# Linear attention and gated convolution FFN on one core: fp32 staging of k, half loads, a split last output tile

## The chip, the cores and the metric

The kernel runs on one core of one Trainium2 chip. The metric is the device time of one execution in microseconds (us); three runs of the kernel before gave a median of 182.67 us (182.66 to 183.72).

## What is computed

The inputs are q, k and v (8 batches, 8 heads, 576 rows, 64 columns, fp32), a norm weight, and the weights of a feed-forward block. The attention is linear, without a softmax, and its output goes through an RMS norm over the 64 columns of a head. The block is a product, a ReLU, a depthwise convolution of three taps along the sequence, a sigmoid gate and a second product.

```python
kv = np.einsum('bhsd,bhse->bhde', k, v)
out = np.einsum('bhsd,bhde->bhse', q, kv)
rms = np.sqrt(np.mean(out * out, axis=-1, keepdims=True) + 1e-06)
x = out / rms * g_norm                      # heads side by side: (8, 576, 512)
h = np.maximum(x @ w_in, 0.0)               # w_in 512 x 1024
conv_out = sum(conv_w[k] * hp[:, k:k + S, :] for k in range(3))   # hp: h padded by one row at each end
gate = 1.0 / (1.0 + np.exp(-conv_out))
result = (h * gate) @ w_out                 # w_out 1024 x 512
```

## The kernel before

**A written order.** The kernel is a list of steps, ORDER, one token for each; the tokens are walked in turn, and each calls a small function (an `@op`) that issues the step's instructions. After the walk the instructions of each engine are chained in the order in which they were issued, so that every engine runs its own in exactly that order, and also the DMA issues of POOL and SP. Across engines only data and buffers hold a step back. In a token such as `om.0.2.1@3` the name is the step, the numbers are its arguments, the digits behind `@` choose the buffer that a new tile takes, and `!A` or `!V` choose ACT (ScalarE) or DVE (VectorE) for a copy or a ReLU.

**Buffers.** There are four PSUM buffers of two banks (names with "a"), two SBUF buffers each for q, k, v and for h, five for o32, and a few for each of the other tiles. A tile that takes a used buffer waits until all readers of the tile before it have finished. Four "row" buffers hold output rows until they are stored.

**Loads.** POOL loads q, k and v from fp32 memory into bf16 tiles, with the cast in the DMA (`load`, L347 and L349); `Lq.b`, `Lk.b` and `Lv.b` load a whole batch, 576 KB as bf16, and `Lq.b.u` one half of it (u = 0 or 1, four heads each). `Li.j` loads a quarter of w_in, `Lo.i` a half of w_out. The first halves of batch 0 do not come this way: in `pre` (L244), SP loads them as fp32 into the tile `stg` (L249), and the steps `ca` (L373) cast them on ACT and DVE, one quarter each.

**Attention.** For batch b: `kv` is the product of k and v (whole, or one half), `kvc` its copy from PSUM to bf16, `qt` transposes one half of q on PE and `qc` copies it, `ot` gives the attention output for one half, `sq` its squares on ACT.

**Norm.** Batches 0 and 1 go tile by tile: `on` sums the squares with a matrix of ones, `nl` takes the reciprocal root on ACT, `mz` scales on DVE. The other batches go in pairs, 2 and 3, 4 and 5, 6 and 7 (groups 1, 2, 3): `oc` copies the output to fp32, `ss` sums the squares of both batches into one tile, `ln` takes the reciprocal root, `sl` splits it into two bf16 parts in four DVE instructions, `sp` spreads it with small matmuls, and `mu` scales (eight for a pair). ACT changes its function table between the root and the sigmoid.

**Feed-forward.** `hm` multiplies one batch with one block of 128 columns of w_in, over one half of x, with `re` as the ReLU; for the pairs 2/3 and 4/5, `ha` and `hb` do it over both batches at once (512 columns, and the 128 left over), with `rea` and `reb`. On DVE `ta` makes the two side taps, `aa` and `ab` add them up, `mg` multiplies h by the gate, in place; `sg` is the sigmoid on ACT. The convolution runs over batch 0, batch 1, pairs 2/3 and 4/5, batch 6 and batch 7 (chunks 0 to 5); `mg.5.1` is the last of its products. `om.p.k.i` is half of the second product (four of the eight blocks of 128 of the inner dimension) for output tile k of pair p. A tile is 128 or 256 output rows of 512 columns; for pair 3 tiles 2 to 6 are single, and tile 6 is the last. `ea` (L643) copies the finished tile to a row buffer and `st` (L647, L650) stores it from SP.

**Zero-matmuls.** `fi`, `fn`, `fq` and `fo` multiply zeros, into a PSUM tile that is overwritten later; they only keep PE busy in waits.

**Around the change.** At the start PE runs the zero-matmuls, transposes the first half of q of batch 0, forms the first half of kv, and then needs the second halves, which POOL casts in the order q, k, v. Batches 2 to 7 are loaded whole. `om.0.2.0` stands ahead of `ss.2` and `ss.3`, the statistics of batches 2 and 3. The last three PE steps are `om.3.6.1`, `om.3.4.0` and `om.3.6.0`, four matmuls of 512 columns each.

Of the kernel before, what the change touches and what calls it, by code (L numbers as in the profile page):

```python
# [59 lines left out]
HALF = [0, 1]  # L60
# [3 lines left out]
OMT = {0: [(0, 1), (2, 3), (4, 5), (6, 7), (8,)], 1: [(0, 1), (2, 3), (4, 5), (6, 7), (8,)], 2: [(0, 1), (2, 3), (4, 5), (6, 7), (8,)], 3: [(0, 1), (2, 3), (4,), (5,), (6,), (7,), (8,)]}  # L64
TAPS = 2
# [15 lines left out]
mg.0.0 hm.1.7.0@1 hm.1.6.0@3 hm.1.7.1 qc.2.0!V@1 hm.1.2.0@2 hm.1.2.1 ta.0.6@1 sg.0.3 ta.0.7 re.1.2!A hm.1.6.1 re.1.6!A
hm.1.1.0@0 hm.1.4.0@2 hm.1.4.1 hm.1.5.0@3 sg.0.2 re.1.7!A hm.1.5.1 Lo.0 aa.0.3 kv.2@1 ab.0.3 re.1.4!A sg.0.6 sg.0.7
hm.1.1.1 re.1.5!A mg.0.1 ta.1.6@0 hm.1.0.0@2 hm.1.0.1 Lk.3@1 ta.1.7 kvc.2!V aa.1.3 re.1.1!A re.1.0!A ot.2.0@1,3
sq.2.0@0 mg.0.3 Lv.3@1 ta.1.4@1 hm.1.3.0@0 ab.1.3 oc.2.0@4 sq.2.1@1 ta.1.5 hm.1.3.1 re.1.3!V oc.2.1 om.0.1.0@2 aa.1.2
sg.1.7 ab.1.2 sg.1.6 mg.1.3 ta.1.0@0 ta.1.1 ot.2.1@1,3 sq.2.2@2 oc.2.2@0 sg.1.4 oc.2.3 sq.2.3@3 om.0.0.0@0 kv.3@1
kvc.3!V aa.1.0 ab.1.0 ot.3.1@1,3 Lo.1 fo.3.384.3.3 om.0.1.1 sg.1.5 oc.3.2@1 mg.1.2 Lq.5@1 oc.3.3 ta.1.3@1 ta.1.2
aa.1.1 sg.1.1 sq.3.2@4 om.0.0.1 qt.3.0@1 ea.0.1!A@0 sg.1.0 ab.1.1 mg.1.0 Lv.4@0 qt.5.1@2 sq.3.3@5 sg.1.3 Lk.4@0
qc.5.1!V@3 qc.3.0!V@2 om.0.2.1@3 sg.1.2 ot.3.0@2,1 ea.0.0!A@1 st.0.0 mg.1.1 sq.3.1@6 sq.3.0@7 om.0.2.0 ss.2@0 ss.3
ea.0.2!V@2 ln.1@0 Lv.5@1 kv.4@0 kvc.4!A oc.3.1@2 oc.3.0 om.0.3.1@3 sl.1@0 sp.2.0.1@0 sp.2.1.0@1 mu.2.1.0@1 mu.2.0.1
sp.3.1.1@2 mu.3.1.1 om.0.3.0 sp.2.0.0@1 mu.2.0.0 sp.2.1.1@0 qt.5.0@2 ea.0.3!A@3 qc.5.0!A@1 mu.2.1.1 sp.3.0.1@3 Lk.5@1  # L90
kv.5@1 mu.3.0.1 kvc.5!A Lq.4@0 sp.3.0.0@0 mu.3.0.0 sp.3.1.0@2 ot.5.1@3,1 sq.5.3@0 fo.2.384.5.2 ha.1.2.0@0 Lk.6@0
oc.5.3@3 mu.3.1.0 ot.5.0@2,1 ha.1.2.1 sq.5.2@1 oc.5.2 ha.1.3.0@3 Lv.7@0 oc.5.1@4 ha.1.3.1 rea.1.2!V@1 oc.5.0 sq.5.1@2
# [34 lines left out]
def kernel(  # L127
# [116 lines left out]
    def pre():  # L244
# [3 lines left out]
        for x in "qkv":  # L248
            nc.sync.dma_start(out=T["stg"][:, "qkv".index(x)], in_=rows(x, 0, 0, 2))  # L249
# [459 lines left out]
```

## Time and profile before

| | |
|---|---|
| median of three runs | 182.67 us |
| the profiled execution | 182.64 us, its span (first to last instruction) 180.9 us |
| matmuls on PE | 2238, of which 288 are the second product (65.4 us busy) |
| mean granted TensorE clock | 0.997 |
| POOL's load queue | 15.38 MB, 51.4% of 16 DMA engines over the span |
| SP's queue (staging and stores) | 11.21 MB, 16.6% |
| the three staging transfers, 576 KB each | 3.7, 4.7 and 5.8 us from issue to landing |
| longest waits on POOL | q loads, 18.7 us for PE's transposes; v loads, 11.8 us for kv |

Times count from the span's start unless they are durations. Engines are PE (matmuls), PEld (its weight loads, beside PE), DVE, ACT, POOL and SP. A line such as L638 is the line that issued an instruction; copies and ReLUs are issued by helpers, so L218 and L220 (copies), L224 and L226 (ReLUs) and L349 (loads) stand for many steps, and the tile's name and shape tell which. A wait on the page is put down to what ended it last.

### The profile page before, as it was taken

Reading aid. Unit: us, or ns where it says so; the run is one execution under the profiler, and the core shown is the slowest. Engines: PE = TensorE matmul, PEld = TensorE weight load, DVE = VectorE, ACT = ScalarE, POOL = GpSimd, SP = SyncE. Lnnn points to the kernel's source line nnn. Section 1 sums busy time; section 2 is a strip of 40 time slices with the busy share of each in tenths; the row PEclk is TensorE's granted clock in tenths of the full one; section 3 lists DMA queues with packets and bytes.
Section 4 is the critical chain, followed back from the end, with each engine's and each line's share of the span. In section 5 each row is a group of like instructions: output and inputs, shape, how many; then the busy total and the mean of one; then the engine's idle time right before and its main releaser. Section 6 shows DMA issues by size and latency. Waiting matters only on the chain.

```text
span 180.9 us, 5152 instructions
## 1 busy us (share of the span) xinstructions
PE 169.5 (94%) x2238; PEld 93.6 (52%) x2238; DVE 153.0 (85%) x268; ACT 139.8 (77%) x196; POOL 27.5 (15%) x49
## 2 busy tenths in 40 slices
PE   7987998899899889999999999999999999999991
PEld 7734754576344444545545564443477754444440
DVE  2656899999996695699999999999999989998840
ACT  2447499999999658999999999995999955755302
POOL 6964165103111311300000000000000000000000
PEclk9999999999999999999999999999999999999998
DMA  5999999999999999999019000004330000550694
GB/s 191 269 189 204 199 207 210 205 207 208 206 209 207 257 207 209 208 203 157 6 71 332 6 4 2 4 0 174 118 120 0 0 0 4 198 208 0 232 364 158
DMA packets 20954, 26.91 MB, mean 149 GB/s; under 512 B 952, under 2 KB 15556, under 8 KB 20932
## 3 DMA queue, kind: packets, MB, share of 16 engines
q0 software_dynamic: 15152, 15.38, 51.4%
q1 hardware_dynamic: 5776, 11.21, 16.6%
q8 instruction: 17, 0.28, 0.6%
q14 instruction: 5, 0.04, 0.1%
q10 hardware_dynamic: 4, 0.00, 0.0%
HBM read 32.52 MB, written 9.44 MB: 232 GB/s over the span
## 4 chain that ended last, share of the span: by engine, by line
PE 46%; DMA 24%; ACT 13%; DVE 9%; POOL 3%; issue 2%; POOLq 0%; ACTq 0%
PE om_ps L638 20%; DMA v_sb<-in_v_dram 15%; PE h_ps L526 10%; PE h_ps L539 10%; DMA k_sb<-in_k_dram 9%; ACT sq L440 3%; DVE xT L510 2%; ACT h L224 2%; ACT o L218 2%; ACT taps L620 2%; PE kv_ps L387 2%; PE h_ps L554 2%; DVE taps L588 2%; DVE taps L582 1%; ACT L213 1%
## 5 line engine op out<-in xcount | busy, mean ns | idle before, releaser
L638 PE MATMUL om_ps<-w_out_sb,h 128*128 128x512 bf16 x288 | 65.4, 379 | 0.0
L620 ACT ACTIVATE taps<-taps,cw 128x576 bf16<-128x576 bf16 (+1 forms) x48 | 43.8, 942 | 9.4 <-DVE taps L588 9.3
L638 PEld LDWEIGHTS <-h 128*128 128x128 bf16 x288 | 27.3, 98 | 32.2 <-issue 1.2
L224 ACT ACTIVATE h<-h_ps 128x576 bf16<-128x576 f32 (+2 forms) x44 | 32.0, 767 | 4.0 <-PE h_ps L526 3.1
L526 PE MATMUL h_ps<-xT,w_in_sb 128*128 128x288 bf16 x256 | 33.7, 286 | 0.4 <-DVE xT L510 0.2
L539 PE MATMUL h_ps<-xT,w_in_sb 128*128 128x512 bf16 x128 | 29.8, 380 | 0.1
L526 PEld LDWEIGHTS <-w_in_sb 128*128 128x128 bf16 x256 | 24.5, 98 | 8.4 <-issue 1.3
L218 ACT ACTIVATE row<-om_ps 128x1024 f32<-128x1024 f32 (+1 forms) x16 | 14.1, 887 | 12.4 <-PE om_ps L638 12.3
L588 DVE TENSOR_TENSOR taps<-taps,h 128x1152 bf16<-128x1152 bf16 (+1 forms) x24 | 22.9, 955 | 0.5
L440 ACT ACTIVATE sq<-o_ps 128x576 bf16<-128x576 f32 x32 | 20.5, 670 | 3.8 <-PE o_ps L433 3.6
L582 DVE TENSOR_TENSOR taps<-taps 128x1152 bf16<-128x1152 bf16 (+1 forms) x24 | 23.0, 956 | 0.4
L626 DVE TENSOR_TENSOR h<-h,taps 128x1152 bf16<-128x1152 bf16 (+1 forms) x24 | 22.7, 951 | 0.0
L575 DVE TENSOR_SCALAR taps<-h,cw 128x576 bf16<-128x576 bf16 (+1 forms) x48 | 20.0, 417 | 1.6 <-ACT h L224 1.6
L576 DVE TENSOR_SCALAR taps<-h,cw 128x576 bf16<-128x576 bf16 (+1 forms) x48 | 20.3, 422 | 0.0
L510 DVE SCALAR_TENSOR_TENSOR xT<-o,cw,sp_ps 128x576 bf16<-128x576 f32 x24 | 17.9, 808 | 1.6 <-PE sp_ps L503 1.6
L539 PEld LDWEIGHTS <-w_in_sb 128*128 128x128 bf16 x128 | 11.8, 98 | 13.9 <-issue 1.4
L218 ACT ACTIVATE o<-o_ps 128x576 f32<-128x576 f32 x24 | 15.6, 687 | 0.0
L213 ACT ACT_TABLE_LOAD x8 | 10.3, 1283 | 2.1 <-issue 2.0
L349 POOL DMA_DIRECT2D q_sb<-in_q_dram x9 | 6.8, 752 | 25.5 <-PE qt_ps L412 18.7
L220 DVE COPY qT<-qt_ps 128x1152 bf16<-128x1152 bf16 x11 | 8.2, 753 | 1.9 <-PE qt_ps L412 1.9
L226 DVE TENSOR_SCALAR h<-h_ps 128x576 bf16<-128x576 f32 (+1 forms) x8 | 6.9, 870 | 2.9 <-PE h_ps L539 2.1
L220 DVE COPY row<-om_ps 128x1024 f32<-128x1024 f32 (+1 forms) x6 | 5.7, 956 | 4.1 <-PE om_ps L638 3.3
(75 smaller groups left out, 140.0 us busy)
## 6 DMA issues: line engine op xcount, KB each, us to landing
out_dram<-row SPq DMA_DIRECT2D x14, 512.0 KB, 3.4
q_sb<-in_q_dram POOLq DMA_DIRECT2D x6, 576.0 KB, 12.0
v_sb<-in_v_dram POOLq DMA_DIRECT2D x6, 576.0 KB, 13.5
k_sb<-in_k_dram POOLq DMA_DIRECT2D x6, 576.0 KB, 15.2
out_dram<-row SPq DMA_DIRECT2D x8, 256.0 KB, 2.3
w_in_sb<-in_moe_w_in_dram POOLq DMA_DIRECT2D x4, 256.0 KB, 10.2
w_out_sb<-in_moe_w_out_dram POOLq DMA_DIRECT2D x2, 512.0 KB, 17.9
q_sb<-in_q_dram POOLq DMA_DIRECT2D x3, 288.0 KB, 8.6
```

Source lines behind the costliest of these rows:

```text
L218: nc.scalar.activation(to, fr, AX.Copy)
L224: nc.scalar.activation(to, fr, AX.Relu)
L440: nc.scalar.activation(by_r(s), natural(T["ot", b, t][:, :S]), AX.Square)
L510: nc.vector.scalar_tensor_tensor(x_tile(b)[:, 2 * tp:2 * tp + 2, at], T["o32", b, tp][:, :, at], g_sb, T["sp", b, tp, e][:, :, :HS], op0=A ...
L526: nc.tensor.matmul(ps[:, e, :HS], w_in_sb[:, t, f * P:(f + 1) * P], x[:, t, e * HS:(e + 1) * HS], start=(t == 0), stop=(t == NT - 1))
L539: nc.tensor.matmul(ps[:, e], w_in_sb[:, t, f * P:(f + 1) * P], x[:, t, e * 512:(e + 1) * 512], start=(t == 0), stop=(t == NT - 1))
L576: nc.vector.tensor_scalar_mul(tap[:, 1, f % 2, :n, :S], h[:, f], cw[:, 2 * NF + f:2 * NF + f + 1])
L582: nc.vector.tensor_add(tap[:, 1, :, :n, :S], tap[:, 0, :, :n, 7:7 + S], tap[:, 1, :, :n, 1:1 + S])
L588: nc.vector.tensor_add(y, y, h[:, 2 * j:2 * j + 2])
L620: nc.scalar.activation(y, y, AX.Sigmoid, scale=scale)
L626: nc.vector.tensor_mul(h, h, T["tap", c, j][:, 1, :, :n, :S])
L638: nc.tensor.matmul(ps[:, j], h[:, f, m * P:(m + 1) * P], w_out_sb[:, f, :], start=first and f == 4 * i, stop=not first and f == 4 * i + 3)
```

## The change

There are four edits. First, the second half of k of batch 0 is loaded by SP as fp32 into a new staging tile, `stg2`, issued right behind the three transfers of `stg`, and cast by two more `ca` steps; the POOL load `Lk.0.1` is gone. Second, batches 1 to 5 are loaded in halves (batches 0 and 1 were before), and `kv` runs by halves for them; POOL issues 38 loads of q, k and v instead of 27. Third, the last output tile (pair 3, tile 6) is computed in two column halves: each takes all eight blocks of the inner dimension and 256 columns, and has its own copy and its own store. Fourth, the order of all steps is new. With it, the stores of pair 0's first four tiles go out in pieces of 256 KB, and two tokens `sw` (a function that was there and unused) make the next store wait for a load: `st.0.1` for k of batch 4, `st.0.2` for v of batch 6.

The diff, cut; of the order three places are shown: the start, the statistics of batches 2 and 3, and the end.

```diff
-HALF = [0, 1]
+HALF = [0, 1, 2, 3, 4, 5]
...
+FIRST = 'k'
+HALFOUT = (3, 6)
+STORES2 = [(0, 1), (0, 2), (0, 0), (0, 3)]
...
-pre@0,0,0 ca.q.0!V Lq.0.1 ca.q.1!V fi.36.128@1 fi.3.128@1 qt.0.0@0 qc.0.0!A@0 ca.k.0!V ca.v.0!V ca.v.1!A ca.k.1!V
-fi.1.512@2 fi.20.128@2 ct@1 fq.2.512.kv.0.0@2 fq.1.256.kv.0.0 kv.0.0 Lk.0.1 pc fi.3.512@0 fi.2.128@0 qt.0.1@3 Lv.0.1
-qc.0.1!V@1 kvc.0.0!A ot.0.0@0,2 sq.0.0@0 sq.0.1@1 Lq.1.1@1 fn.3.512.on.0.0@1 fn.2.128.on.0.0 on.0.0 nl.0.0@0 pn Li.2
-fn.1.512.on.0.1@3 on.0.1 nl.0.1 mz.0.1@0 Li.0 fo.2.384.0.0 kv.0.1@1 kvc.0.1!A fq.1.512.ot.0.1@3 fq.1.256.ot.0.1
...
+pre@0,0,0 ca.q.1!V ca.q.0!A fi.9.512@1 fi.1.128@1 qt.0.0@0 pn Lq.0.1 ca.k.1!V qc.0.0!A@0 Lv.0.1 ca.k.0!V fi.6.512@2
+fi.2.128@2 ct@1 ca.v.1!A ca.v.0!V fq.1.512.kv.0.0@2 fq.1.256.kv.0.0 kv.0.0 kvc.0.0!A fq.2.512.ot.0.0@3 ot.0.0@0
+sq.0.1@0 fn.3.512.on.0.1@2 fn.2.128.on.0.1 on.0.1 ca.k.2!V sq.0.0@1 pc Lq.1.0@1 nl.0.1@0 fo.1.384.0.0 qt.0.1@1
+qc.0.1!V@1 Li.2 on.0.0@2 ca.k.3!A mz.0.1@0 fo.3.384.0.0 kv.0.1@1 nl.0.0 kvc.0.1!V fq.2.512.ot.0.1@2 ot.0.1@0 qt.1.0@1
...
+qt.2.0@3 mz.1.1 nl.1.0 qc.2.0!A@4 fq.1.512.ot.1.1@1 fq.1.256.ot.1.1 ot.1.1@2 sq.1.3@6 mz.1.0 Lq.3.1@1 aa.0.3
+fo.2.384.1.2 kv.2.0@3 on.1.3@0 Lq.2.1 sq.1.2@7 kvc.2.0!A fo.2.384.1.3 on.1.2@3 nl.1.3@3 nl.1.2 fo.1.384.1.2 hm.1.6.0@0
...
-qc.5.1!V@3 qc.3.0!V@2 om.0.2.1@3 sg.1.2 ot.3.0@2,1 ea.0.0!A@1 st.0.0 mg.1.1 sq.3.1@6 sq.3.0@7 om.0.2.0 ss.2@0 ss.3
-ea.0.2!V@2 ln.1@0 Lv.5@1 kv.4@0 kvc.4!A oc.3.1@2 oc.3.0 om.0.3.1@3 sl.1@0 sp.2.0.1@0 sp.2.1.0@1 mu.2.1.0@1 mu.2.0.1
...
+om.0.2.1@3 ea.0.0!V@1 sq.3.0@6 sq.3.1@7 ss.2@2 ss.3 sg.1.2 sg.1.3 mg.1.1 ln.1@0 Lv.5.1@0 sl.1@0 oc.3.0@2 Lk.5.0@0
+om.0.2.0 Lk.5.1 kv.5.1@2 oc.3.1 qt.5.0@0 sp.3.0.1@1 kvc.5.1!V sp.2.0.0@2 ea.0.2!A@2 mu.3.0.1@1 mu.2.0.0 qc.5.0!A@4
+om.0.3.0@3 sp.2.1.1@1 mu.2.1.1 sp.2.1.0@0 sp.3.1.1@2 om.0.3.1 Lq.4.0 mu.2.1.0 mu.3.1.1 Lq.5.1 sp.3.1.0@1 sp.2.0.1@0
+Lv.5.0 mu.2.0.1 qt.5.1@2 ea.0.3!A@3 sp.3.0.0@3 mu.3.1.0 mu.3.0.0 qc.5.1!A@2 Lk.4.0@1 kv.5.0@0 kvc.5.0!A Lv.4.0@1
+Lk.4.1 qt.4.0@1 sw.k.4 st.0.1 qc.4.0!V@1 ot.5.1@2,0 sq.5.2@0 sq.5.3@1 ha.1.2.0@3 ha.1.2.1 ha.1.3.0@1 Lv.4.1 oc.5.2@3
+Lq.7@1 oc.5.3 rea.1.2!V@0 ot.5.0@2,0 oc.5.1@0 ha.1.3.1 rea.1.3!V hb.1.0@3 sq.5.0@2 oc.5.0 sq.5.1@3 kv.4.1@2 kvc.4.1!V
+reb.1.0!A kv.4.0@1 fq.1.256.ot.4.1@0 ot.4.1@2 kvc.4.0!A sq.4.2@4 oc.4.3@4 ta.2.2@0 Lv.6@0 sq.4.3@5 ha.1.0.1@3 oc.4.2
...
-om.3.3.1@2 sg.5.0 om.3.2.1@0 sg.5.2 mg.5.0 st.2.1 mg.5.1 om.3.3.0 om.3.2.0 ea.3.0!V@0 st.3.0 ea.3.3!V@1 ea.3.2!V@2
-om.3.5.0 om.3.4.1@1 st.3.1 st.3.2 st.3.3 om.3.6.1@2 ea.3.5!V@0 st.3.5 om.3.4.0 ea.3.4!A@3 st.3.4 om.3.6.0 ea.3.6!A@2
-st.3.6
...
+sg.5.5 om.3.0.0@0 om.3.0.1 re.7.1!V om.3.1.1 ab.5.1 sg.5.4 mg.5.2 sg.5.2 st.2.1 st.2.3 ea.3.0!A@1 st.3.0 ta.5.0@1
+ea.3.1!A@2 ta.5.1 aa.5.0 ab.5.0 sg.5.0 om.3.2.1@3 om.2.2.0 sg.5.1 mg.5.0 st.3.1 sg.5.3 om.3.5.1@0 om.3.3.1@2
+ea.2.2!A@3 st.2.2 mg.5.1 om.3.3.0 om.3.2.0 st.2.4 om.3.4.0@1 ea.3.2!V@1 ea.3.3!A@2 st.3.3 om.3.5.0 ea.3.5!A@3 st.3.2
+om.3.6.1@2 st.3.5 ea.3.6.1!A@0 st.3.6.1 om.3.4.1 ea.3.4!A@2 st.3.4 om.3.6.0 ea.3.6.0!A@1 st.3.6.0
...
+        if FIRST:
+            T["stg2"] = work.tile([P, len(FIRST), 2, S], FP32, name="stg2", tag="h0", bufs=1)
+            for i, x in enumerate(FIRST):
+                nc.sync.dma_start(out=T["stg2"][:, i], in_=rows(x, 0, 2, 2))
...
-        copy(eng, qkv(x, 0)[:, w, :], T["stg"][:, "qkv".index(x), w])
+        fr = T["stg"][:, "qkv".index(x), w] if w < 2 else T["stg2"][:, FIRST.index(x), w - 2]
+        copy(eng, qkv(x, 0)[:, w, :], fr)
...
+        if (p, k) == HALFOUT:
+            at = slice(i * 256, (i + 1) * 256)
+            for f in range(NF):
+                nc.tensor.matmul(
+                    ps[:, i, :256], h[:, f, ms[0] * P:(ms[0] + 1) * P], w_out_sb[:, f, at],
+                    start=(f == 0), stop=(f == NF - 1))
+            return
...
-    def ea(p, k, eng):
-        copy(eng, tl(("os", p, k), "row", [P, len(OMT[p][k]), D_model], FP32, "row"), T["om", p, k])
+    def ea(p, k, c=None, eng=None):
+        if c is None:
+            copy(eng, tl(("os", p, k), "row", [P, len(OMT[p][k]), D_model], FP32, "row"), T["om", p, k])
+        else:
+            copy(eng, tl(("os", p, k, c), "row", [P, 1, 256], FP32, "row"), T["om", p, k][:, c:c + 1, :256])
...
+        step = 1 if (p, k) in STORES2 else n
+        for j in range(0, n, step):
+            st = nc.sync.dma_start(
+                out=out_rows[at + j * P:at + (j + step) * P, to].rearrange("(j p) m -> p j m", p=P),
+                in_=fr[:, j:j + step])
+            for x in hold:
...
```

## The prediction

> **What bounds the kernel now.** I read the page's slices first, then the stretches, then the chain of waits, then the order in time around the places that the change touches.
>
> ```profile
> PE 169.5 (94%) x2238; PEld 93.6 (52%) x2238; DVE 153.0 (85%) x268; ACT 139.8 (77%) x196; POOL 27.5 (15%) x49
> ...
> DMA  5999999999999999999019000004330000550694
> GB/s 191 269 189 204 199 207 210 205 207 208 206 209 207 257 207 209 208 203 157 6 71 332 6 4 2 4 0 174 118 120 0 0 0 4 198 208 0 232 364 158
> ```
>
> The loads keep the DMA engines full until about 85 us, at 200 to 210 GB/s of bf16 written (the fp32 read is twice that); after that DMA is idle but for stores.
>
> ```profile
> 17.36:58.79 41.43, 39.36 (x681) 23.40 (x681) 38.10 (x74) 38.33 (x59) 10.53 (x15) 1.00 1.23 207
> 56.98:75.01 18.03, 16.30 (x370) 8.65 (x367) 10.84 (x16) 12.94 (x21) 2.96 (x4) 1.00 1.20 220
> 75.01:169.95 94.94, 94.51 (x875) 49.44 (x874) 92.21 (x144) 80.92 (x106) 1.64 (x2) 1.00 0.31 89
> ```
>
> Columns: stretch, length, busy PE, PEld, DVE, ACT, POOL, clock, DMA share, GB/s. Three regimes: up to 17.36 PE runs mostly zero-matmuls and waits; from 17.36 to 58.79 PE, DVE and ACT are all over 92%; from 75.01 to 169.95 PE is full and DVE is at 97%. Only between 56.98 and 75.01 does DVE idle (7.2 us) and PE lose 1.7 us.
>
> ```profile
> 5.80 7.95 DMA v_sb<-in_v_dram
> ...
> 17.36 2.27 PE h_ps L526 x16
> ...
> 49.75 16.93 DMA k_sb<-in_k_dram
> ...
> 154.41 22.46 PE om_ps L638 x104
> ...
> 176.94 0.60 ACT row L218
> ```
>
> The chain (start, length, what) hangs on batch 0's second half of v, later on loads, and ends in PE, one eviction and its store. Within the open stretch:
>
> ```profile
> 58.79 0.67 PE L476 MATMUL ss_ps<-sq,sel 128*32 128x288 bf16 x16
> 60.20 0.77 PE L387 MATMUL kv_ps<-v_sb,k_sb 64*64 64x64 bf16 x72 [0.73 <-ACT rs L484]
> ```
> ```profile
> 61.42 0.52 DVE L494 SCALAR_TENSOR_TENSOR wparts<-hi,nab,rs 128x288 bf16<-128x288 bf16 x1
> 63.09 4.44 DVE L510 SCALAR_TENSOR_TENSOR xT<-o,cw,sp_ps 128x576 bf16<-128x576 f32 x6 [1.15 <-PE sp_ps L503]
> ...
> 71.25 1.22 DVE L226 TENSOR_SCALAR h<-h_ps 128x1024 bf16<-128x1024 f32 x1 [1.93 <-PE h_ps L539]
> ...
> 75.01 0.52 DVE L575 TENSOR_SCALAR taps<-h,cw 128x1152 bf16<-128x1152 bf16 x1 [0.84 <-ACT h L224]
> ```
>
> This is the norm of batches 2 and 3: statistics (ss), root (ln), split (sl), spread (sp), scaling (mu), first joint products (ha), relu, first taps at 75.01 (ta.2.2). It is a latency chain, and little else is left for DVE.
>
> The profiled execution took 182.64 us (span 180.9 plus 1.7 around it), against a median of 182.67; sums go against 182.64.
>
> **Totals that do not change.** I counted the order's steps and priced each by its form's row, or by start-to-start spacing where instructions overlap (0.54 for a 128x576 ACT step of 0.67). Products, squares, taps and sigmoids are the same in number. ACT and DVE differ in casts (1 and 5 before, 3 and 5 after), kvc (7 and 3; 5 and 9, mostly halves), qc (5 and 11; 6 and 10), relus (44 and 8; 42 and 10) and evictions (16 and 6; 21 and 2). By that PE's work is the same within 0.7 us, DVE's 0.9 us less, ACT's 3 us more: two casts of about 0.6 in the start, the rest at the end, where the page's ACT digits are 3 to 7. Eight table loads before and after. Zero-matmuls have 26,880 and 28,544 columns; they fill waits. So all gain or loss is idle time moved.
>
> **Start (k's second half by SyncE).** Before, three 576 KB fp32 transfers, then q, k, v halves as casts: landings at about 10.9, 12.3, 13.8 us (issue 4.37, 5.09, 5.80 plus 6.5, 7.2, 8.0). The k cast goes; a fourth fp32 transfer comes ahead of it. Both read 576 KB of fp32 source, so six such reads precede v's landing before and after; the streams run at 397 GB/s fp32 (5 to 6 us) and about 200 bf16, that is 400 read. Queue work alone therefore gives nothing. But in 7 to 10 us the casts ramp up at 130, 141 and 172 GB/s, 157 KB or 0.8 us short of 200; the fourth transfer can fill that. Gain 0 to 0.8; nothing in the rows makes sharing free or costly, so a loss of up to 0.5 stays as an end. I take 0.4. Behind v the stream is the same: kv.0.1, kvc, ot, squares, norm, first h product took 17.36 - 13.89 = 3.47 us and will again. SP's new issue (0.5 us by the row of its neighbours) stands behind the other three; nothing on SP waits before 57 us. The new DVE cast (0.46 to 0.64) stands ahead of pc (about 1.8) and qc (0.75) in DVE's order: if k lands at L, qT is ready at L + 3.0, needed about 14.9, so it costs nothing until L passes 12; I put L at 9 (alone) to 11.6 (shared evenly).
>
> **Halves.** POOL issues 38 instead of 27 q/k/v loads at 0.74 us: 8 us on an engine 15% busy, hidden as long as the queue holds work, which at full DMA share it does. Halves land 1.45 us apart above; full loads at 207 GB/s need 2.85, so a half costs at most 0.03 more: eight extra before batch 5's k, 0.2 us, inside about 2 us of slack. I take 0.
> The Trainium skill ("DMA: Bandwidth & Descriptors", Anatomy of one DMA) speaks against halves: about 2 us fixed for each transfer, so, it says, batch to 1 MiB. By that, unoverlapped, eight extra loads would be an estimated 16 us. The spacing above does not bear it out while the queue is full.
> What halves buy is kv and qt of single halves, so that om.0.2.0 can go behind ss instead of ahead of it.
>
> **The open stretch.** PE has 1.4 us less real work ahead of ss.3 (one om half, 8 x 0.214 = 1.7, moved behind). But after the last square ACT now runs two sigmoids (2 x 0.68), a table load (1.28) and the root (0.50), where before the table load ran ahead; by ACT's sum (0.6 us more up to ln.1, of which 1.2 lies in its early idle) ln.1 ends 0.6 us earlier, not 1.4. From the end of sl to ta.2.2 before: 75.01 - 61.94 = 13.1. After: sp stands directly behind qt.5.0, so the 1.15 us wait shrinks to some 0.5; eight mu at 0.75 with two short gaps, 7.0; then four ha halves (0.85 each, the first already possible when batch 2's mu are done), ot, hb, relu, about 4.8: together 11.8. So ta.2.2 comes 1.9 earlier if nothing else stalls, 0.6 if only ln moves, 2.4 if ACT isn't the limit. DVE gets one more relu (1.2) here; I take 1.4.
>
> **From ta.2.2 to the end.** DVE's sum to the last mg.5.1: 91.0 against 91.1. PE's products behind mg.5.1: seven quarter-tile pieces at 0.85, 6.0, as before, and before PE came 0.9 us late to them. The last sigmoids now leave DVE nothing to do (its 1.22 us eviction went to ACT), up to 0.9 us, which that slack covers. PE stands 1.2 us further in its own list at ta.2.2. Ends -1.2 and +1.0; I take 0.
>
> **Tail.** PE ends 176.86; the last eviction, 128x512 on ACT, 0.60, becomes 128x256, nearest row 0.38: -0.2. The last store, 256 KB at 307 to 389 GB/s, 0.7 to 0.85, becomes 128 KB: -0.4. Sixteen 256-column matmuls have the columns of eight of 512, and as many weight loads again, hidden (PEld under half). -0.6, ends -0.2 and -0.9.
>
> **Stores and late loads.** SP now waits for k of batch 4 ahead of st.0.1, and for v of batch 6 ahead of st.0.2; all later stores stand behind. Who needs them are ea.0.4 (st.0.1's row) and ea.1.0 (st.0.2's). By the stream (1.43 us for each half) k of batch 4 lands about 52 us behind v.0.1 and v of batch 6 about 60 to 62; by PE's sum those evictions come at about 70 and 88. A store beside loads cost the casts 1.45 us before (60 to 64 us: 268 and 257 GB/s for 207, so 222 of the store's 524 KB were extra and 300 KB were displaced); it now falls where the stream has a gap, because q of batch 7 waits for qt.5.1, some 3 us. The kv.7 that needs these loads is 5 us off. 0, by that cover; each us beyond it costs one.
>
> Sum: 0.4 + 0 + 1.4 + 0 + 0.6 = 2.4 us; 182.64 - 2.4 = **180.2 us**.
>
> **Rivals.**
> A, no change: the open stretch's gain is eaten, because PE and DVE are full from 75 us on and DVE's chain, with 1.7 us more work ahead of ta.2.2 by its sum, arrives no earlier; only the tail stays. 182.0, from 181.2 to 183. For it: DVE at 97%, three full engines from 17 to 58 us that any small wait hits. Against: 7.2 us of DVE idle to draw on. 0.32.
> B, slower: PE works in order, and kv.2.0 and kv.5.1 now stand ahead of on.1.3 and of the sp's; if each extra half delays the stream by g, PE stands there 8g - 2. It beats the gains from g = 0.55 and is 1% slower from 0.8; at 0.9, 185.4. For it: POOL already waits at each issue in the first 17 us. Against: 1.45 us spacing. 0.08.
> By the fixed cost that the Trainium skill's page ("DMA: Bandwidth & Descriptors") states, B would be the outcome.
> C, the edit doesn't do what it says: k's fp32 transfer runs ahead of q and v in full and pushes them 1.4 us, nothing regained. That is the end 0 of the first term, 180.6, inside the forecast's range.
>
> The forecast has 0.60, own range 178.6 to 181.4. About 1% (1.8 us) is what this measurement can tell from none. Faster by more needs under 180.8: 0.52 of the 0.60, 0.02 of A: 0.54. Within 1%: 0.08 + 0.30 + 0.01 = 0.39. Slower: 0.07. Range 178.6 to 183.0: it leaves out B and the best ends.
>
> **What would show it.** Start: kv.0.1 at 13.1 to 13.9. Halves: full DMA slices to about 83 us at over 200 GB/s. Stretch: ta.2.2 (first 128x1152 taps) near 73.2; DVE idle ahead of it under 6 us. End: 6.0 to 6.9 us from the last mg to PE's end, then 3.5 instead of 4.0 to the span's end. Wrong, if DMA slices before 80 us show gaps, if PE waits for DMA at kv.2.0 or kv.5.1, or if PE idles over 1 us after 75 us.

## The result, and the profile after

The changed kernel takes 180.47 us (median of four runs, 180.00 to 180.96), against 182.66 for the kernel before (182.60 to 183.72): a ratio of 0.9876, 95% interval 0.9831 to 0.9922, so 1.2% faster (0.8 to 1.7% by the interval); the prediction took 1% as the bound. Its profiled execution took 180.49 us, with a span of 178.7.

The page of the kernel after: busy time of TensorE, the DMA engines' busy tenths and the rate, in 40 slices of 4.47 us.

```profile
PE 169.0 (95%) x2206; PEld 91.3 (51%) x2206; DVE 151.5 (85%) x271; ACT 143.4 (80%) x200; POOL 34.7 (19%) x60
...
DMA  5999999999999999999970000001075000242674
GB/s 196 357 200 198 204 207 205 207 205 207 208 206 207 209 226 152 206 185 254 172 269 6 0 6 0 0 4 59 0 274 201 0 0 0 94 189 72 235 293 176
```

TensorE's busy time is 0.45 us less, mostly in zero-matmuls. The second slice moved 357 GB/s where before it moved 269: the fp32 transfer of k fills the ramp of the casting loads. The last load lands at 89.4 us, and from 67 to 71 us the stream is thin (152 GB/s).

Three stretches of the kernel after, the columns as in the prediction: up to the statistics of batches 2 and 3 (`ss.2`, now at 56.27), the 18 us ahead of the first taps of the pair (`ta.2.2`, now at 73.04), and from there to `mg.5.1`.

```profile
55.01:73.04 18.03, 17.28 (x373) 9.14 (x370) 13.10 (x19) 13.12 (x21) 2.95 (x4) 1.00 1.12 197
16.49:56.27 39.78, 37.98 (x678) 23.01 (x677) 37.94 (x76) 37.54 (x59) 18.64 (x27) 1.00 1.23 206
73.04:169.04 96.00, 94.62 (x883) 49.75 (x880) 92.75 (x144) 82.17 (x106) 2.22 (x3) 1.00 0.36 100
```

DVE is idle for 4.9 us in the open stretch instead of 7.2, TensorE for 0.75 instead of 1.7. The long stretch behind it lasts 96.0 us where it lasted 94.9: DVE has 0.54 us more work in it and waits 0.5 us more.

The open stretch in the order of time, first TensorE, then DVE:

```profile
56.27 0.67 PE L486 MATMUL ss_ps<-sq,sel 128*32 128x288 bf16 x16
56.88 1.90 PE L655 MATMUL om_ps<-w_out_sb,h 128*128 128x512 bf16 x8
...
59.74 0.42 PE L513 MATMUL sp_ps<-wparts,spread 32*128 32x288 bf16 x4 [0.23 <-DVE wparts L504]
...
65.64 0.48 PE L397 MATMUL kv_ps<-v_sb,k_sb 64*64 64x64 bf16 x36
66.18 0.48 PE L422 MATMUL qt_ps<-ident,q_sb 64*64 64x64 bf16 x36
66.47 0.57 PE L443 MATMUL o_ps<-qT,kvw 64*64 64x64 bf16 x8
66.98 2.76 PE L549 MATMUL h_ps<-xT,w_in_sb 128*128 128x512 bf16 x12
```
```profile
60.15 1.54 DVE L520 SCALAR_TENSOR_TENSOR xT<-o,cw,sp_ps 128x576 bf16<-128x576 f32 x2 [0.35 <-PE sp_ps L513]
62.27 4.58 DVE L520 SCALAR_TENSOR_TENSOR xT<-o,cw,sp_ps 128x576 bf16<-128x576 f32 x6 [0.58 <-PE sp_ps L513]
...
71.12 1.22 DVE L230 TENSOR_SCALAR h<-h_ps 128x1024 bf16<-128x1024 f32 x1 [0.98 <-PE h_ps L549]
...
73.04 0.52 DVE L585 TENSOR_SCALAR taps<-h,cw 128x1152 bf16<-128x1152 bf16 x1 [0.19 <-ACT h L228]
```

`om.0.2.0` (56.88) now runs behind the statistics, in the time in which ACT and DVE work on the root, and the wait of 0.73 us that TensorE had there is gone. The first taps come 1.97 us earlier. In TensorE's list `kv.5.0`, `qt.4.0` and `ot.5.1` stand ahead of the first joint product, which starts at 66.98.

Where TensorE was idle in the kernel after, in six stretches (length, busy time, clock, DMA share, GB/s):

```profile
0.00:20.00 20.00, 17.26 (x276) 1.00 1.07 235
20.00:45.00 25.00, 23.79 (x523) 1.00 1.23 206
45.00:75.00 30.00, 28.83 (x506) 1.00 1.15 201
75.00:90.00 15.00, 13.99 (x230) 1.00 1.09 212
90.00:165.00 75.00, 74.63 (x621) 1.00 0.18 67
165.00:178.70 13.70, 10.53 (x57) 1.00 0.61 230
```

Length less busy time gives TensorE's idle time. Beside the same stretches of the trace before, the whole difference of the two spans comes out:

| us | before | after | difference |
|---|---|---|---|
| idle, 0 to 20 | 3.14 | 2.74 | -0.40 |
| idle, 20 to 45 | 1.33 | 1.21 | -0.12 |
| idle, 45 to 75 | 2.46 | 1.17 | -1.29 |
| idle, 75 to 90 | 0.07 | 1.01 | +0.94 |
| idle, 90 to the end of its work | 0.37 | 0.37 | 0 |
| TensorE's busy time | 169.49 | 169.04 | -0.45 |
| end of TensorE (176.86; 175.53) to end of span | 4.04 | 3.17 | -0.87 |
| span | 180.9 | 178.7 | -2.2 |

The open stretch and the tail gain; 75 to 90 us gives 0.9 us back, most of it in one wait of the kernel after, for DVE's ReLU `rea.1.1`, which frees the PSUM buffer that `qt.7.1` takes:

```profile
79.68 0.80 PE L422 MATMUL qt_ps<-ident,q_sb 64*64 64x64 bf16 x72 [0.68 <-DVE h L230]
```

The tail, in ACT's and TensorE's last lines:

```profile
174.74 0.60 ACT L222 ACTIVATE row<-om_ps 128x512 f32<-128x512 f32 x1 [0.53 <-PE om_ps L655]
175.56 0.38 ACT L222 ACTIVATE row<-om_ps 128x256 f32<-128x256 f32 x1 [0.23 <-PE om_ps L649]
```
```profile
174.49 1.04 PE L649 MATMUL om_ps<-w_out_sb,h 128*128 128x256 bf16 x8
```

The 0.87 us has three parts. From the end of TensorE to the issue of the last store it is 0.45 us instead of 0.71, since the last copy takes 0.38 instead of 0.60. From there to the landing of the store, which has half the bytes, it is 1.80 instead of 2.02. Behind the landing it is 0.91 instead of 1.29; this third part is not the tile's, as the experiments show.

**How to compare traces here.** Executions of one kernel start unevenly. The first half of kv (`kv.0.0`), which waits for the cast of a staging transfer, began anywhere from 8.4 to 9.3 us in the profiled executions of kernels with the new order, and the end of TensorE moved with it: from `kv.0.0` to the end of TensorE it was 166.9 to 167.0 us in five of them, whether it began at 8.5 or at 9.3. So below, dates are compared inside a trace, and times by their ratio to the kernel before, which was run beside each group of experiments on the same chip (medians 182.70, 182.51, 182.61 and 182.50). Behind a time stand its lowest and highest run, behind a ratio its 95% interval.

### The profile page after: what moved, and what is told of

The parts are those of the page before. It is cut to its first block, busy times and chain, and to the rows that moved or that the text cites. A ratio compares the mean times of both kernels' runs of the same rounds, so it can differ in the third digit from the quotient of the medians.

```text
span 178.7 us, 5121 instructions
## 1 busy us (share of the span) xinstructions
PE 169.0 (95%) x2206; PEld 91.3 (51%) x2206; DVE 151.5 (85%) x271; ACT 143.4 (80%) x200; POOL 34.7 (19%) x60
## 4 chain that ended last, share of the span: by engine, by line
PE 37%; ACT 29%; DVE 21%; DMA 5%; issue 4%; POOL 2%; POOLq 0%; ACTq 0%
PE om_ps L655 22%; PE h_ps L536 10%; ACT taps L630 8%; ACT h L228 7%; DMA q_sb<-in_q_dram 5%; ACT sq L450 5%; ACT o L222 4%; DVE xT L520 3%; DVE taps L585 3%; DVE taps L586 3%; DVE taps L598 2%; DVE taps L592 2%; ACT L217 2%; DVE h L636 2%; DVE h L230 1%
## 5 line engine op out<-in xcount | busy, mean ns | idle before, releaser
L655 PE MATMUL om_ps<-w_out_sb,h 128*128 128x512 bf16 x280 | 63.5, 379 | 0.3 <-DVE xT L520 0.3
L655 PEld LDWEIGHTS <-h 128*128 128x128 bf16 x280 | 26.6, 98 | 31.9 <-issue 2.1
L228 ACT ACTIVATE h<-h_ps 128x576 bf16<-128x576 f32 (+2 forms) x42 | 30.6, 770 | 3.7 <-PE h_ps L536 3.5
L222 ACT ACTIVATE row<-om_ps 128x1024 f32<-128x1024 f32 (+2 forms) x21 | 17.7, 844 | 12.1 <-PE om_ps L655 9.2
L585 DVE TENSOR_SCALAR taps<-h,cw 128x576 bf16<-128x576 bf16 (+1 forms) x48 | 20.8, 434 | 1.8 <-ACT h L228 1.8
L586 DVE TENSOR_SCALAR taps<-h,cw 128x576 bf16<-128x576 bf16 (+1 forms) x48 | 20.4, 425 | 0.0
L358 POOL DMA_DIRECT2D v_sb<-in_v_dram x13 | 9.4, 720 | 18.6 <-PE kv_ps L397 13.3
L358 POOL DMA_DIRECT2D q_sb<-in_q_dram x13 | 9.4, 721 | 14.8 <-PE qt_ps L422 11.0
L230 DVE TENSOR_SCALAR h<-h_ps 128x576 bf16<-128x576 f32 (+2 forms) x10 | 8.8, 878 | 2.4 <-PE h_ps L549 2.4
L358 POOL DMA_DIRECT2D k_sb<-in_k_dram x12 | 8.7, 724 | 3.6 <-PE kv_ps L397 1.7
```

The lines of the kernel that those rows point to most:

```text
L222: nc.scalar.activation(to, fr, AX.Copy)
L228: nc.scalar.activation(to, fr, AX.Relu)
L358: loads[x, b] = nc.gpsimd.dma_start(out=qkv(x, b)[:, w0:w0 + n, :], in_=rows(x, b, w0, n))
L585: nc.vector.tensor_scalar_mul(tap[:, 0, f % 2, :n, 8:8 + S], h[:, f], cw[:, f:f + 1])
L655: nc.tensor.matmul(ps[:, j], h[:, f, m * P:(m + 1) * P], w_out_sb[:, f, :], start=first and f == 4 * i, stop=not first and f == 4 * i + 3)
```

## The experiments

**The kernel after, once more** (no edit), on the chip of three other runs: the last tile whole, k back on POOL, and `rea.1.1` earlier on DVE.

> The changed kernel itself, so that the other runs of this chip have a yardstick: 180.5 us, within 0.5; span 178.7; kv.0.1 at 13.1, ta.2.2 at 73.0, last mg at 169.0, PE's end at 175.5, 3.2 us from there to the span's end.

180.90 us (180.46 to 181.17), ratio 0.9896 (0.9882 to 0.9910). The first taps were at 72.98 and TensorE ended at 175.50, both within 0.1 of the first profile.

**The last tile whole again.**

```diff
-HALFOUT = (3, 6)
+HALFOUT = None
...
-ea.3.6.1!A@0 st.3.6.1 om.3.4.1 ea.3.4!A@2 st.3.4 om.3.6.0 ea.3.6.0!A@1 st.3.6.0
+om.3.4.1 ea.3.4!A@2 st.3.4 om.3.6.0 ea.3.6!A@1 st.3.6
```

> The changed kernel with its last output tile whole again (two halves of the inner dimension, one copy of 128x512, one store of 256 KB). My theory: eviction and store each get their old size back, so the time from PE's end to the span's end goes from 3.2 back to 4.0 us and the kernel takes 181.3 us (+0.85). Rival: the tail is the fixed latency of a store, and only the eviction counts (+0.2): 180.7 us.

181.46 us (180.92 to 181.54), ratio 0.9922 (0.9909 to 0.9935), 0.56 us above the kernel after on the same chip. From the end of TensorE (176.10) to the end of the span (179.8) it is 3.7 us instead of 3.2. The split of the last tile is worth 0.5 to 0.6 us, a third less than the 0.87 that the two profiles differ by. The three parts tell why: the first two are back (0.66 us to the issue of the store, 2.02 to its landing), the third is not (0.97). Behind the last landing, all nine profiles with the new order have 0.91 to 0.97 us and all five with the old one 1.21 to 1.29, with the split or without; what makes that difference was not tried.

**k's second half back on POOL.**

```diff
-FIRST = 'k'
+FIRST = ''
...
-pn Lq.0.1 ca.k.1!V
+pn Lq.0.1 Lk.0.1 ca.k.1!V
```

and without `ca.k.2` and `ca.k.3`.

> The changed kernel with k's second half of batch 0 cast by POOL's DMA again, between q and v; its two casts on ACT and DVE gone. My theory: v lands at 13.8 instead of 13.0, kv.0.1 and all behind it 0.85 later, nothing behind it has room to make that up: 181.3 us. Rival: later waits (loads, the norm of batches 2 and 3) take it up, so the first h product is late but ss of batches 2 and 3 is not: 180.5 us.

180.99 us (180.63 to 181.50), ratio 0.9907 (0.9890 to 0.9924): 0.1 us above the kernel after by the medians, 0.2 by the ratios, with intervals that overlap. In its trace `kv.0.1` waits 0.30 us for v, and from `kv.0.0` to the end of TensorE it is 167.38 us against 166.9 to 167.0. So the move is worth 0.1 to 0.2 by time and 0.4 by one trace; the 0.85 us of the theory is not there.

**k's second half by SP, in the kernel before alone.**

```diff
+FIRST = 'k'
...
-kv.0.0 Lk.0.1 pc fi.3.512@0
+kv.0.0 pc ca.k.2!V fi.3.512@0
...
-nl.0.0@0 pn Li.2
+nl.0.0@0 ca.k.3!A pn Li.2
```

> The kernel before, with only the second half of k of batch 0 moved from GpSimd's casting load to a fp32 transfer on SyncE and two casts; order else unchanged. Theory (k's move alone makes the start shorter, by the wait of 0.25 us for v ahead of kv.0.1 and the transfers that go out earlier): 182.70 - 0.4 = 182.3 us, kv.0.1 some 0.4 to 0.8 us earlier than in the kernel before (13.9). Rival from the run that gave k back to GpSimd (only +0.1 us): the move is worth 0.1 us and the earlier first product came from the new order of the casts and of the work around kv.0.1: 182.6 us, kv.0.1 still 5.2 to 5.4 us after kv.0.0. A second rival: the DVE cast of k stands ahead of other casts and the time grows, 183.0 us.

182.59 us (182.15 to 183.04), ratio 1.0007 (0.9994 to 1.0019). The ramp of the transfers is filled (344 GB/s in the second slice), and yet `kv.0.1` comes 5.20 us behind `kv.0.0`, as before (5.33). First the row of the kernel before, then that of this kernel:

```profile
13.89 0.67 PE L387 MATMUL kv_ps<-v_sb,k_sb 64*64 64x64 bf16 x36 [0.25 <-DMA v_sb<-in_v_dram]
```
```profile
14.41 0.47 PE L392 MATMUL kv_ps<-v_sb,k_sb 64*64 64x64 bf16 x35 [0.39 <-ACT k_sb L219]
```

It now waits 0.39 us for ACT's cast of k, where it waited 0.25 us for v. Nothing is gained; the transfers' gain stops at the place of a cast in ACT's list.

**Half loads, in the kernel before alone.**

```diff
-Lq.3@0 mg.0.2 kv.1.1@0 Lq.2@1
+Lq.3.0@0 Lq.3.1 mg.0.2 kv.1.1@0 Lq.2.0@1 Lq.2.1
```

and so on for every load of batches 2 to 5.

> The kernel before, with the loads of batches 2 to 5 cut into two halves each that are issued one behind the other where the whole load stood: twelve more transfers, kv still made of whole batches, order else unchanged. Theory (cutting a load costs nothing while the queue is full): 182.7 us, at most 183.0. Rival (each half has a price g of its own in the stream): the load that the end of the open stretch waits for comes 12 g later; with g = 0.25 us that is 3 us, of which 1 us is covered, so 184.7 us; with 2 us for each, which the Trainium skill gives as the fixed cost (page DMA: Bandwidth & Descriptors), 12 x 2 = 24 us and over 200 us. Another rival: GpSimd, which issued no load before the eighth load ahead of it had landed, has half as many bytes under way and leaves gaps in the DMA record around 30 to 60 us; 183 to 185 us.

182.44 us (182.24 to 183.10), ratio 0.9997 (0.9981 to 1.0013). The page of this kernel:

```profile
DMA  5999999999999999999028000004330000550694
GB/s 198 265 193 204 198 207 209 203 206 207 205 208 207 256 206 208 208 208 161 9 84 320 6 4 2 4 0 174 118 120 0 0 0 4 201 206 0 232 365 158
```

The slices are as full as before, and the statistics of batches 2 and 3 start at 58.85 (58.79). Twelve more transfers cost nothing measurable here, at most 0.24 us by the interval (0.0013 of 182.51). By the fixed 2 us for each transfer that the Trainium skill gives ("DMA: Bandwidth & Descriptors", Anatomy of one DMA — SWDGE (gpsimd) path) it would have been an estimated 24 us, had none of it overlapped; these runs, with the queue full, do not agree. The other rival, that half as many bytes under way leave gaps, falls too. In every profile POOL has at most eight loads under way: none goes out less than 0.28 us behind the landing of the eighth load ahead of it, with halves most follow it by less than 0.7 us, and the slices stay full all the same.

**Whole loads in the kernel after**, each at the place of its first half; `kv` still by halves.

```diff
-Lq.2.0@0 mg.0.2 fq.1.512.kv.1.1@1 kv.1.1 kvc.1.1!V Lk.2.0@0
+Lq.2@0 mg.0.2 fq.1.512.kv.1.1@1 kv.1.1 kvc.1.1!V Lk.2@0
```

and the second halves of batches 2 to 5 gone.

> The kernel after, with the loads of batches 2 to 5 whole again, each at the place of its first half; K'V still by halves. Theory (the halves let kv.2.0 and the others run earlier): kv.2.0, which has the first half of k and v of batch 2 just in time at 32.07 us, now waits for whole loads of k, q and v of batch 2, some 3 x 1.4 = 4 us more, and the sum of squares of batches 2 and 3 starts some 1 to 3 us later than 56.2: 181.8 to 183.5 us. Rival (only the order matters, the halves' bytes arrive in time either way since the bytes of batches 2 and 3 are complete by about the same time): 180.6 to 181.0 us.

185.49 us (185.31 to 185.77), ratio 1.0169 (1.0153 to 1.0185): 4.6 to 5.0 us above the kernel after, more than either had it. TensorE at `kv.2.0`, which has no wait in the kernel after:

```profile
35.70 0.69 PE L396 MATMUL kv_ps<-v_sb,k_sb 64*64 64x64 bf16 x36 [3.73 <-DMA v_sb<-in_v_dram]
```

That wait is what was expected. The rest is in the granted clock (columns: stretch, length, TensorE busy, clock, DMA share, GB/s):

```profile
33.50:34.00 0.50, 0.00 (x0) 1.00 1.24 231
34.00:34.50 0.50, 0.00 (x0) 0.54 1.19 196
34.50:35.50 1.00, 0.00 (x0) 0.50 1.20 202
35.50:36.00 0.50, 0.30 (x24) 0.50 1.24 214
36.00:40.00 4.00, 4.00 (x46) 0.50 1.21 207
40.00:40.50 0.50, 0.50 (x3) 0.50 1.22 210
40.50:41.00 0.50, 0.50 (x3) 0.64 1.20 205
41.00:42.00 1.00, 1.00 (x9) 1.00 1.22 211
```

TensorE stops at 31.97. By the means of the two mixed rows the clock falls to a half at 34.04 and is whole again at 40.86, after 5.2 us of work at half speed. `kv.2.0` is 3.63 us later than in the kernel after, `ss.2` 5.34 us (61.61 for 56.27), so the slow clock cost another 1.7 us; between these two steps TensorE waits for only 0.35 us, less than in the kernel after (0.49). The first taps come at 78.34, 5.30 us later than in the kernel after, and TensorE ends at 180.83, also 5.30 us later. Together with the run before it: halves alone give nothing, the new order with whole loads in the places of the first halves loses 5 us, the two together win. Other places for whole loads in this order were not tried.

**The split last tile, in the kernel before alone.**

```diff
+HALFOUT = (3, 6)
...
-st.3.5 om.3.4.0 ea.3.4!A@3 st.3.4 om.3.6.0 ea.3.6!A@2
+st.3.5 ea.3.6.1!A@1 st.3.6.1 om.3.4.0 ea.3.4!A@3 st.3.4 om.3.6.0 ea.3.6.0!A@2
```

> The kernel before, with only its last output tile made in two column halves, copied and stored one after the other. Theory by the trace of after (end of TensorE to end of span 3.2 instead of 4.0 us): 182.70 - 0.85 = 181.85 us. Rival by the run with a whole last tile (0.56 us slower): 182.70 - 0.5 = 182.2 us. Rival 2 (the eight half-wide products cost more than the tail gives back): 182.7 us.

183.46 us (182.83 to 183.85), ratio 1.0049 (1.0031 to 1.0066): 0.95 us slower, as no theory had it. ACT's and TensorE's lines at the end of this kernel:

```profile
177.20 0.87 ACT L219 ACTIVATE row<-om_ps 128x256 f32<-128x256 f32 x2 [7.73 <-DMA out_dram<-row]
```
```profile
177.63 1.03 PE L641 MATMUL om_ps<-w_out_sb,h 128*128 128x256 bf16 x8 [1.20 <-ACT row L219]
```

The copy of the first half takes row buffer 1 and waits for the store that holds it (by the order, `st.3.3`); TensorE's last eight products then wait for that copy.

**The same with a fifth row buffer.**

```diff
-ea.3.6.1!A@1 st.3.6.1
+ea.3.6.1!A@4 st.3.6.1
```

> The kernel before with its last output tile in two column halves, as in the run that came out 0.9 us slower, but the first half has a fifth row buffer of its own. Theory (there ACT's copy of the first half waited for a store to free its row buffer, and TensorE waited for that copy 1.2 us): both waits are gone, the end of TensorE to the end of the span is 3.2 us, and the time is 182.6 - 0.5 to 0.85 = 181.75 to 182.1 us. Rival (the split costs as such, by its half-wide products or its seventh store): 183 us or more.

181.98 us (181.66 to 182.13), ratio 0.9965 (0.9953 to 0.9977): 0.63 us faster than before. Both waits are gone. So the split gives the same 0.6 us in either order, if its copy finds a free row buffer; the kernel after gives it buffer 0, and ACT's copies at its end wait only for TensorE.

**`om.0.2.0` ahead of the statistics, in the kernel after.**

```diff
-sq.3.0@6 sq.3.1@7 ss.2@2 ss.3 sg.1.2 sg.1.3 mg.1.1 ln.1@0
+sq.3.0@6 sq.3.1@7 om.0.2.0 ss.2@2 ss.3 sg.1.2 sg.1.3 mg.1.1 ln.1@0
...
-om.0.2.0 Lk.5.1 kv.5.1@2
+Lk.5.1 kv.5.1@2
```

> The kernel after, with the eight products om.0.2.0 put back ahead of ss.2 and ss.3, as the kernel before has them; nothing else moved. By the trace of after the statistics start 1.8 us later (58.1 instead of 56.3), the root some 1.5 us later since ACT's table load then ends ahead of them (58.8 instead of 57.3), and TensorE, which has one half tile less to do behind them, waits some 1.6 us for sp. Theory (the date of the norm of batches 2 and 3 passes to the end one to one): first taps at 74.5, 180.6 + 1.5 = 182.1 us. Rival (DVE and TensorE are full from 75 us on and take up the delay, as in rival A of the prediction): first taps at 74.5, but 180.6 to 180.9 us.

At this place `om.0.2.0` reads two of its four blocks of h before `mg.1.1` has gated them, and `mg.1.1` waits until it has read them; the number of instructions is the same. 182.41 us (181.48 to 183.47), ratio 0.9987 (0.9960 to 1.0015), so 1.5 to 1.9 us above the kernel after. TensorE in this kernel, then DVE's first taps:

```profile
58.38 0.68 PE L486 MATMUL ss_ps<-sq,sel 128*32 128x288 bf16 x16
59.66 0.48 PE L397 MATMUL kv_ps<-v_sb,k_sb 64*64 64x64 bf16 x36 [0.60 <-ACT rs L494]
...
61.55 0.42 PE L513 MATMUL sp_ps<-wparts,spread 32*128 32x288 bf16 x4 [0.87 <-DVE wparts L504]
```
```profile
74.84 0.52 DVE L585 TENSOR_SCALAR taps<-h,cw 128x1152 bf16<-128x1152 bf16 x1 [0.19 <-ACT h L228]
```

The taps are 1.80 us later than in the kernel after (73.04), and TensorE ends 1.80 us later (177.33 for 175.53). Of this 0.3 us was there before the moved step (`kv.3.0` at 51.42 for 51.12); 1.5 is the move. The date of this norm goes to the end one to one, as it did with whole loads (5.30 and 5.30 us); the rival's 180.6 to 180.9 us is out. The opposite edit, `om.0.2.0` behind the statistics in the kernel before, was not tried.

**`rea.1.1` earlier on DVE**, ahead of `ab.2.1`:

```diff
-sq.4.0@6 ab.2.1 sq.4.1@7 oc.4.0@1 ha.1.4.0@3 ss.4@2 rea.1.1!V ss.5
+sq.4.0@6 rea.1.1!V ab.2.1 sq.4.1@7 oc.4.0@1 ha.1.4.0@3 ss.4@2 ss.5
```

> The changed kernel with one DVE step moved: the ReLU rea.1.1 ahead of ab.2.1 instead of behind it, so that PE's transpose qt.7.1 finds its PSUM buffer free. If PE's list sets the end from 75 us on, its 0.68 us wait ahead of qt.7.1 goes and the kernel takes 179.9 us. Rival: DVE's list sets the end, and PE waits the same time at a later step that needs DVE: 180.4 us.

180.71 us (180.29 to 182.74), ratio 0.9903 (0.9865 to 0.9940). The wait of 0.68 us is gone, and TensorE waits 0.67 us for DVE 6.8 us later:

```profile
86.44 1.89 PE L655 MATMUL om_ps<-w_out_sb,h 128*128 128x512 bf16 x8 [0.67 <-DVE xT L520]
```

From the first taps to the end of TensorE it is 102.28 us instead of 102.49: the wait has moved to a later step, as the rival had it.

**`rea.1.1` on ACT.**

```diff
-ha.1.4.0@3 ss.4@2 rea.1.1!V ss.5 oc.4.1 ln.2@0 qt.7.1@1 qt.7.0@0 ha.1.4.1 qc.7.1!A@0
+ha.1.4.0@3 rea.1.1!A ss.4@2 ss.5 ln.2@0 oc.4.1 qt.7.1@1 ha.1.4.1 qt.7.0@0 qc.7.1!A@0
```

> The kernel after, with the ReLU rea.1.1 on ACT instead of DVE, ahead of ln.2, with oc.4.1 behind ln.2 and one step of TensorE (ha.1.4.1) ahead of qt.7.0. Theory (from 73 to 92 us DVE is without a gap, and its list delays TensorE: 1.0 us of idle between 75 and 90 where before had 0.1): with 1.2 us less on DVE the wait of 0.68 us ahead of qt.7.1 falls to about 0.3, the scaling of batches 4 and 5 comes 0.4 us earlier, and the time is 0.3 to 0.6 us less: 180.1 to 180.4 us. Rival (ACT is as full there, and delays the root ln.2 by as much): 180.7 us, or slower, up to 181.2 us.

180.70 us (180.03 to 181.13), ratio 0.9891 (0.9872 to 0.9909). `qt.7.1` waits 0.24 us instead of 0.68, but from the first taps to the end of TensorE it is 102.43 us. Taking 1.2 us from DVE here changed nothing: the rival's price.

**Stores not held back.** The tokens `sw.k.4` and `sw.v.6` are left out.

```diff
-Lk.4.1 qt.4.0@1 sw.k.4 st.0.1
+Lk.4.1 qt.4.0@1 st.0.1
...
-qc.7.1!A@0 sw.v.6 st.0.2
+qc.7.1!A@0 st.0.2
```

> The kernel after, without the two waits of SyncE that hold st.0.1 and st.0.2 back for loads; stores go out as soon as their rows are ready. Theory (no one waits for a row buffer, so the waits cost nothing, and what the early stores take from the loads, some 300 KB or 1.45 us, is covered by the gap of the stream at 65 to 70 us): 180.7 us, within 0.3. Rival (the stores push the loads of batches 4 to 7, and TensorE waits for kv.5.0 or kv.4.1): 181.2 to 182.2 us.

180.00 us (179.94 to 180.60), ratio 0.9868 (0.9854 to 0.9881), below both forecasts and the lowest time of the study, but its interval meets that of the kernel after (0.9831 to 0.9922 in the first runs, 0.9882 to 0.9910 in the second). Its traced start was also the earliest (`kv.0.0` at 8.42), and from there to the end of TensorE it is 166.69 us, 0.2 less than in the five traces above. The stores now lie in the load stream from 52 us (251 and 255 GB/s for 207 and 226), the loads end at about 87 us, and TensorE waits for no load. The waits buy nothing here; whether they cost 0.3 us is not settled.

## Why the prediction was right, step by step

The time (180.2 against 180.47) and the sum (2.4 against 2.2 us) were right. The terms were not all right, and that the sum came so near is in part luck. By the dates of the first two profiles the first taps come 1.97 us earlier (forecast 1.8), the segment from there to the end of TensorE is 0.64 longer (forecast 0), and the tail is 0.87 shorter (forecast 0.6). The loss of 0.64 had no term; it was covered in part by taps that came a little earlier than forecast, and by 0.38 us behind the last landing that had no term either.

**Start, 0.4: not borne out by the times.** In the old order the move cost 0.1 us (-0.1 to +0.35 by the interval); taken back in the new one it was worth 0.1 to 0.2, though the intervals there do not exclude 0.4. The mechanism at the queue was as described, 357 for 269 GB/s, and it gave more than forecast: v's second half landed at 11.98 to 13.14 us in the nine profiles with k by SP and at 13.48 to 13.99 in the five with k by POOL. But little of this reaches the products. The step "the new DVE cast costs nothing until L passes 12" was about the wrong cast: the other one, `ca.k.3`, stands in ACT's list, and in the old order `kv.0.1` waited for that. In the new order that cast ran at 11.99 instead of 13.69, and `kv.0.1` came at 13.06 without a wait, 0.36 us behind v's landing, since TensorE still had zero-matmuls to run. The sign (13.1 to 13.9) was a little too late. The first feed-forward product came 0.87 us earlier in the first two profiles (16.49 for 17.36), but its date varies from 16.34 to 17.59 between the kernels with the new order.

**Halves, 0: right.** As a cost they are 0 (0.9997). Rival B fell with that. Their use, that they allow another order, is worth more than was said: without them the new order loses 5 us.

**Open stretch, 1.4: right in size, wrong in its parts.** The end of `sl.1` came 2.34 us earlier (59.60 for 61.94), where 1.0 was expected (0.4 from the start and 0.6), because ACT began the root 2.34 us earlier. The rows of before and after, with ACT's busy time from the first feed-forward product to that root:

```profile
59.64 0.50 ACT L484 ACTIVATE rs<-ss_ps,eps_sb 128x288 f32<-128x288 f32 x1
17.36:59.64 42.28, 39.17 (x59) 1.00 1.23 207
```
```profile
57.30 0.50 ACT L494 ACTIVATE rs<-ss_ps,eps_sb 128x288 f32<-128x288 f32 x1
16.49:57.30 40.81, 38.56 (x59) 1.00 1.23 206
```

ACT's work in that stretch fell by 0.61 us, just as its sum said (0.6 more in all, 1.2 of it ahead of the stretch). What the step "by ACT's sum ln.1 ends 0.6 us earlier" left out is ACT's idle time, 3.1 us before and 2.2 after; the remaining 0.87 is the date of the first product. The stretch behind it, where 13.1 was to become 11.8, became 13.4. The wait ahead of the scalings shrank to 0.55 us and the eight scalings took 6.7, as costed; but "the first ha already possible when batch 2's mu are done" overlooked TensorE's own list, which has `kv.5.0`, `qt.4.0` and `ot.5.1` ahead of it until 66.98. Two errors of opposite sign, which is luck: in sum -1.97 us at the taps against -1.8.

**From the taps to the end, 0: half right.** That a date of the taps passes to the end is shown (1.80 and 1.80 us with `om.0.2.0` put back, 5.30 and 5.30 with whole loads). So rival A, in which the full engines eat the gain, fell, although its condition, DVE at 97%, held. But the segment itself is longer, 102.49 us from the taps to the end of TensorE against 101.85, and 101.86, 101.87 and 101.87 in three more kernels with the old order. The named sign, TensorE idle over 1 us after 75, came true with 1.4 us, and the prediction had no term for it, though 0.64 lies inside the ends that it gave (-1.2 and +1.0). Both attempts at its largest wait moved it instead of removing it, so what sets this segment is open: DVE's list, ACT's, or the order of TensorE.

**Tail, 0.6: right**, 0.56 and 0.63 by the two experiments; of the 0.87 that the profiles show, 0.38 lies behind the landing and is not the split's. Its parts were mis-sized: the smaller store gave 0.22 us instead of 0.4, the shorter copy 0.26 up to the issue instead of 0.2. That it holds only with a free row buffer was not said.

**Stores, 0: right** in cost. `st.0.1` went out at 65.0 us, when k of batch 4 had landed, and at 51.9 without the wait; its pieces landed by 68.4, and ACT wrote the next rows into that buffer (`ea.0.4`) at 87.6, so nobody waited for SP. The gap of the stream at 65 to 70 us, where POOL waits 9.5 us for `qt.5.1`, was there (190 GB/s); the sign "full slices to 83 us" forgot it, and TensorE never waited for it.

Added up by the times, the pieces give as much as the whole or more: 0.1 to 0.2 (k), 1.5 to 1.9 (statistics ahead of `om.0.2.0`) and 0.5 to 0.6 (tail) are 2.1 to 2.7 us, and the gain is 1.8 to 2.2. The kernel with `om.0.2.0` put back says the same: it has the tail and k by SP, and is only 0.1 us faster than the kernel before. The rest of the new order therefore costs some 0.5 us; the interval of that run (0.7 faster to 0.3 slower than before) allows 0 to 1. Its trace places the cost: from the taps to the end of TensorE it has the same 102.49 us as the kernel after, 0.64 more than the old order. Which step of the new order makes this segment longer was not found.

## What to carry to other kernels

Here the smaller loads were not the gain by themselves, the order that they allowed was, so try each without the other: halves alone gave 0, the order without them lost 5 us, together they gained. In a norm between two full stretches, look for work that can stand behind the statistics instead of ahead of them, since its date may go to the end undiminished. When a tile is split, count the buffers that its extra pieces take: the same split was worth -0.6 or +0.95 us, by one row buffer.

## What the hardware showed unexpectedly

With whole loads, a wait of 3.73 us for a load made the next statistics 5.3 us late. TensorE's granted clock fell to 0.50 some 2.1 us after its last product, and it stayed there for 6.8 us, 5.2 us of them with work; the kernels before and after, without a wait that long, had 0.997 and 1.000 on the mean, and the 0.997 comes from the last 1.1 us of the span, when TensorE had finished. The Trainium skill ("TensorE: Matmul & The Clock Gate", Part 1: The HAM clock gate (the "warmup" mystery)) puts the half clock behind at least one idle window of about 3.4 us, and the full clock behind about 3.4 us of sustained work, with windows that run free of the kernel. The half and the free-running window agree with this trace (6.8 us is two such windows); the fall after only 2.1 us of idle time does not.

All 14 profiles together narrow this down. Every stretch between two changes of the clock is a whole multiple of 3.41 us, and at the end of a profile the clock falls anywhere from 1.3 us (the split last tile in the kernel before) to 4.9 us (stores not held back) after TensorE's last product, so the length of the idle time does not decide by itself. Cut into windows of 3.41 us that end where the clock changes, the traces show the half clock behind every window at full clock in which TensorE worked 1.3 us or less (with whole loads, 30.62 to 34.04), and behind none in which it worked 1.9 us or more; no window lies between.
